# Attention and squared-ReLU MLP on one core: another order for the prologue, eight steps for the attention, loads issued before stores

## The chip, the cores and the metric

The kernel runs on one NeuronCore of one Trainium2 chip. The metric is device time in microseconds (us), lower is better; a run's time is a little longer than the span that its profile shows, since the span goes from the first to the last instruction.

## The reference

q, k and v are 8 x 8 x 576 x 64 (batch, heads, sequence, head size). Attention is local: the sequence is cut into chunks of 64, and a query sees the keys of its own chunk alone. The result, 4608 tokens of 512 channels, goes through an MLP with a squared ReLU:

```
scores = scale * q_c @ k_c^T          (per chunk of 64 and head)
attn   = exp(scores - max);  attn = attn / (sum + 1e-9)
x      = attn @ v_c                   -> (4608, 512)
h = x @ w_in (512 x 2048);  r = max(h, 0);  g = s * r*r + b
out = g @ w_out (2048 x 512)
```

All of it is in float32.

## The kernel before

The 4608 tokens are 36 token blocks (tb) of 128; four of them make a *block* of the outer loop, so there are nine blocks (L311). The hidden size 2048 is cut into 16 parts j. For each block and each j the kernel does an up-projection `up(j)` (L224: 12 matmuls 128 x 512 into one PSUM bank of the pool ps_h, which has two), on ScalarE and VectorE the square (L235) and the bias (L241), which leaves g as a high and a low part, and a down-projection `down(j)` (L248: 12 matmuls that accumulate in ps_o over all j). To keep float32 accuracy, x, the weights and g are each split into a high and a low part of type fp32r, and a product is three matmuls: high x high, low x high, high x low. `down` runs LAG = 2 steps behind `up`, so a block has 18 steps (L322), and `store` (L260) copies the four results out of PSUM on ScalarE and issues four stores on SP.

The weights arrive as 64-bit numbers, and the core converts them itself in block 0. The 32 weight tiles (up and down for each j) are put into 16 pairs (L61). A pair is loaded into one of three buffers of the pool raw; `scale` and `tail` (L87, L91) are on ScalarE, `bits` (L95) is two VectorE instructions (L98, L99) and one on GpSimd (L101), `hi` (L103) is on ScalarE and `lo` (L107, instruction L109) on VectorE. In block 0, step j does lo of pair j, tail and bits of pair j+2, hi of pair j+1, scale and load of pair j+3 (L330 to L343). The raw buffers are shared with the q and k of the attention, so a load waits until the buffer's earlier user has been read.

Attention is done two token blocks at a time, in a *group*: class Attention, L113. Its stages are load_qk, load_v, scores (64 matmuls of 64 x 64, L150), peak (L155), sub (L159), exp (L164), sum (L168), norm (reciprocal and product with it, L171 to L173, on VectorE), transposes (8 on TensorE, L180), copies (ScalarE, L185), values (64 matmuls, L191), x_hi (ScalarE, L201) and x_lo (VectorE, L205). A block needs two groups. While one block's MLP runs, the two groups of the next block are spread over its steps by a table, `plan` (L314 to L321): the key (j, 0) is ahead of up(j), (j, 1) behind up(j), and (j, 2) between the square and the bias of step j. The first group loads at (0, 0), has its scores at (1, 1), its product at (4, 2), transposes at (5, 1), values at (6, 1) and x_lo at (7, 2); the second group is seven steps later. One PSUM tile, ps_a, serves scores, transposes and values of a group in turn.

The first two groups (called one and two), and the first weight pairs, are done in a prologue (L272 to L308).

The order of the work is written out by hand: the pool manager runs with a manual schedule, each engine executes its instructions in the order of the program, and waits are put in where a tile's data or buffer needs them. All DMAs are issued on SP, in order; a DMA that has to wait holds every later one.

The lines that do this in the main loop:

```
for j in range(NJ + LAG):
    run(*plan.get((j, 0), ()))
    ...
layer.store()
```

Of the kernel before, what the change touches and what calls it, by code (L numbers as in the profile page):

```python
# [8 lines left out]
F32 = mybir.dt.float32  # L9
F32R = mybir.dt.float32r  # L10
U32 = mybir.dt.uint32
I32 = mybir.dt.int32
AF = mybir.ActivationFunctionType
ALU = mybir.AluOpType
# [4 lines left out]
def local_attention_then_squared_relu_mlp(ctx: ExitStack, tc, qkv, w, s, b, out):  # L19


    nc = tc.nc
    P = 128
    NTB, NJ = qkv.shape[0], w.shape[0]
# [18 lines left out]
    ps_h = ctx.enter_context(tc.tile_pool(name="ps_h", bufs=2, space=bass.MemoryType.PSUM))  # L43
# [8 lines left out]
    b_col = const.tile([P, 1], F32, name="b_col")  # L52
    ident = const.tile([P, P], F32, name="ident")
    make_identity(nc, ident)

# [6 lines left out]
    class Pair:  # L64
# [27 lines left out]
            _, low, _, _, _ = self.views(which)  # L92
            nc.scalar.activation(out=low.bitcast(I32), in_=low, func=AF.Copy, scale=2.0 ** -29)

        def bits(self, which=(0, 1)):  # L95
            f, low, high, _, _ = self.views(which)
            u, i = f.bitcast(U32), f.bitcast(I32)
            nc.vector.tensor_scalar(out=u, in0=u, scalar1=3, scalar2=None, op0=ALU.logical_shift_left)  # L98
            nc.vector.scalar_tensor_tensor(out=u, in0=high, scalar=0x80000000, in1=u,  # L99
                                           op0=ALU.bitwise_and, op1=ALU.bitwise_or)  # L100
            nc.gpsimd.tensor_tensor(out=i, in0=i, in1=low.bitcast(I32), op=ALU.add)  # L101

        def hi(self, which=(0, 1)):  # L103
            f, _, _, hi, _ = self.views(which)
# [102 lines left out]
    def block(tb0, bank):  # L207
        x = [xp.tile([P, NHP, 4 * P], F32R, name=n) for n in ("xh", "xl")]
        return x, [Attention(tb0 + i, x, i * P, bank) for i in range(0, 4, N)]
# [57 lines left out]
    def run(*steps):  # L267
        for f in steps:
            f()
# [3 lines left out]
    pair = [Pair(k) for k in range(NJ)]  # L273
# [7 lines left out]
    pair[2].load()  # L281
    nc.sync.dma_start(out=s_col, in_=s.unsqueeze(0).to_broadcast([P, 1]))
    nc.sync.dma_start(out=b_col, in_=b.unsqueeze(0).to_broadcast([P, 1]))
    run(one.scores, one.peak, one.sub, two.scores)
    pair[0].scale((0,))
    pair[0].tail((0,))
    one.exp()
    pair[0].bits((0,))
    run(one.sum, one.norm, one.transposes, two.peak, two.sub)
    pair[0].hi((0,))  # L290
    pair[0].scale((1,))
    pair[0].tail((1,))
    run(one.copies, one.values, two.exp)
    pair[0].lo((0,))
    pair[0].bits((1,))
    run(one.x_hi, two.sum, two.norm, two.transposes, one.x_lo)
    layer = Layer(0, x)
    first, second = slice(0, N * P), slice(N * P, 4 * P)
    layer.up(0, first)
    pair[0].hi((1,))  # L300
    run(two.copies, two.values)
    pair[0].lo((1,))
    pair[1].scale()
    pair[1].tail()
    pair[1].bits()
    layer.up(1, first)
    run(two.x_hi, two.x_lo)
    pair[2].scale()  # L308


    for tb0 in range(0, NTB, 4):  # L311


        plan = {}  # L314
        if tb0 + 4 < NTB:
            next_x, groups = block(tb0 + 4, steady_bank)
            for a, n in zip(groups, (1, 8)):
                for at, *fs in (((n - 1, 0), a.load_qk, a.load_v), ((n, 1), a.scores), ((n, 2), a.peak), ((n + 1, 2), a.sub),
                                ((n + 2, 0), a.exp), ((n + 2, 2), a.sum), ((n + 3, 2), a.norm), ((n + 4, 1), a.transposes),
                                ((n + 5, 0), a.copies), ((n + 5, 1), a.values), ((n + 6, 0), a.x_hi), ((n + 6, 2), a.x_lo)):  # L320
                    plan.setdefault(at, []).extend(fs)  # L321
        for j in range(NJ + LAG):  # L322
            run(*plan.get((j, 0), ()))
            if j < NJ:
                if tb0 or j > 1:
                    layer.up(j)
                else:
                    layer.up(j, second)
            run(*plan.get((j, 1), ()))
            if tb0 == 0:  # L330
                if j + 3 < NJ:
                    pair[j + 3].load()
                if 0 < j < NJ:
                    pair[j].lo()
                if j + 2 < NJ:
                    pair[j + 2].tail()
                    pair[j + 2].bits()
                if j + 1 < NJ:
                    pair[j + 1].hi()
            if j < NJ:  # L340
                layer.square(j)
            if tb0 == 0 and j + 3 < NJ:
                pair[j + 3].scale()  # L343
            run(*plan.get((j, 2), ()))
            if j < NJ:
                layer.bias(j)
            if j >= LAG:
                layer.down(j - LAG)
        layer.store()
        if tb0 + 4 < NTB:  # L350
            x = next_x
            layer = Layer(tb0 + 4, x)


# [29 lines left out]
```

## Time and profile before

| | |
|---|---|
| median of 3 runs | 897.93 us (896.51 to 898.06) |
| the profiled execution | 896.87 us, its span 895.1 us |
| mean granted TensorE clock | 0.996 |
| TensorE busy | 859.1 us (96% of the span) |
| VectorE / ScalarE / GpSimd busy | 375.9 / 308.7 / 39.8 us |
| DMA | 55.40 MB, 62 GB/s over the span |

In the rows, PE is TensorE, PEld its weight loads, DVE VectorE, ACT ScalarE, POOL GpSimd, and SPq the queue of SP, which issues the DMAs. A row of the timeline is: start (us), duration (us), engine, line of the kernel, operation, out<-in, shape, count, and in brackets the idle time of the engine just before it with what released it. Durations of a matmul hold its way through the array, so that matmuls overlap: twelve matmuls of 512 columns last 2.72 us from the first start to the next group's start.

### The profile page before, as it was taken

The numbers are of one execution on the slowest core, as the hardware profiler recorded it, in microseconds if no ns is written. First come the engines' busy times: TensorE is split into PE (matmuls) and PEld (weight loads), VectorE is DVE, ScalarE is ACT, GpSimd is POOL, SyncE is SP. The second block draws the span as 40 slices with busy tenths as digits, with TensorE's granted clock in tenths as the row PEclk, the third lists the DMA queues.
The fourth block names the chain that finished last, engine by engine and source line by source line (L and its number), as shares of the span: only waits on it lengthen the run. The fifth ranks groups of instructions, "written<-read, shape, count | busy, mean of one in ns | idle before, by whom it ended". The sixth has DMA issues, their size and how long they took to land.

```text
span 895.1 us, 13596 instructions
## 1 busy us (share of the span) xinstructions
PE 859.1 (96%) x5928; PEld 707.3 (79%) x5928; DVE 375.9 (42%) x483; ACT 308.7 (34%) x466; POOL 39.8 (4%) x23
## 2 busy tenths in 40 slices
PE   4789999999999999999999999999999999999997
PEld 3678787888788878888788878887888788888886
DVE  6698954342334334332534243433343343423221
ACT  4777743223332223232233233223322332322222
POOL 1333310000000000000000000000000000000000
PEclk9999999999999999999999999999999999999999
DMA  7556304000400040001200040004000400010001
GB/s 299 198 187 215 138 9 158 25 1 1 166 22 3 1 164 1 25 1 68 97 25 1 1 165 24 1 1 165 24 2 1 149 17 25 0 47 2 1 1 47
DMA packets 20507, 55.40 MB, mean 62 GB/s; under 512 B 2528, under 2 KB 2528, under 8 KB 20448
## 3 DMA queue, kind: packets, MB, share of 16 engines
q1 hardware_dynamic: 20448, 54.54, 16.8%
q8 instruction: 46, 0.75, 0.3%
q14 instruction: 13, 0.11, 0.0%
HBM read 45.09 MB, written 9.44 MB: 61 GB/s over the span
## 4 chain that ended last, share of the span: by engine, by line
PE 83%; DVE 7%; DMA 6%; ACT 2%; issue 1%; SPq 1%; POOL 0%; ACTq 0%; POOLq 0%
PE ps_o L257 42%; PE ps_h L231 36%; DMA raw<-in_qkv_dram 4%; PE ps_a L180 2%; PE ps_a L191 2%; PE ps_a L150 1%; DVE wp L109 1%; DMA raw<-in_w_dram 1%; DVE f L99 1%; ACT f L264 1%; DVE ps_h L239 1%; DVE f L98 1%; DVE g L245 1%; DVE p L173 1%; DVE z L171 1%
## 5 line engine op out<-in xcount | busy, mean ns | idle before, releaser
L257 PE MATMUL ps_o<-wp,g 128*128 128x512 f32 x1728 | 418.3, 393 | 0.0
L231 PE MATMUL ps_h<-xh,wp 128*128 128x512 f32 (+1 forms) x1168 | 380.9, 389 | 5.3 <-DVE g L245 5.0
L257 PEld LDWEIGHTS ps_o<-wp,g 128*128 128x128 f32 x1728 | 322.4, 188 | 67.1
L239 DVE SCALAR_TENSOR_TENSOR ps_h<-ps_h,s_col,r 128x512 f32<-128x512 f32 x144 | 109.1, 758 | 434.9 <-ACT r L238 434.9
L231 PEld LDWEIGHTS ps_h<-xh,wp 128*128 128x128 f32 x1168 | 219.6, 189 | 51.0 <-issue 4.8
L231 PE MATMUL ps_h<-xl,wp 128*128 128x512 f32 (+1 forms) x584 | 226.5, 388 | 0.8 <-DVE xl L205 0.8
L238 ACT ACTIVATE r<-ps_h 128x512 f32<-128x512 f32 x144 | 86.0, 597 | 387.8 <-PE ps_h L231 387.8
L244 ACT ACTIVATE g<-ps_h,b_col 128x512 fp32r<-128x512 f32 x144 | 99.2, 689 | 116.6 <-DVE ps_h L239 116.6
L245 DVE SCALAR_TENSOR_TENSOR g<-ps_h,b_col,g 128x512 fp32r<-128x512 f32 x144 | 107.4, 746 | 54.2 <-ACT g L244 54.2
L231 PEld LDWEIGHTS ps_h<-xl,wp 128*128 128x128 f32 x584 | 110.4, 189 | 23.0 <-DVE xl L205 1.0
L101 POOL TENSOR_TENSOR f<-f,raw 128x1024 int32<-128x1024 int32 (+1 forms) x17 | 39.1, 2300 | 78.1 <-DVE f L99 47.8
L264 ACT COPY f<-ps_o 128x512 f32<-128x512 f32 x36 | 19.4, 590 | 44.2 <-PE ps_o L257 44.2
L180 PE MATMUL ps_a<-ident,p 128*128 128x128 f32 x144 | 21.1, 295 | 10.6 <-DVE p L173 10.6
L180 PEld LDWEIGHTS ps_a<-ident,p 128*128 128x128 f32 x144 | 18.3, 153 | 13.5 <-issue 11.7
L150 PEld LDWEIGHTS ps_a<-raw 64*64 64x64 f32 x1024 | 17.2, 134 | 14.6 <-DMA raw<-in_qkv_dram 7.5
L150 PE MATMUL ps_a<-raw 64*64 64x64 f32 x1024 | 20.2, 222 | 8.0 <-DMA raw<-in_qkv_dram 7.6
L89 ACT ACTIVATE f<-raw 128x1024 f32<-128x1024 f32 (+1 forms) x17 | 18.6, 1094 | 15.6 <-DMA raw<-in_w_dram 11.9
L155 DVE TENSOR_REDUCE m<-ps_a 128x16 f32<-128x1024 f32 x16 | 19.5, 1219 | 7.8 <-PE ps_a L150 7.8
L109 DVE TENSOR_TENSOR wp<-f,wp 128x1024 fp32r<-128x1024 f32 (+1 forms) x17 | 22.3, 1313 | 0.0
L173 DVE TENSOR_TENSOR p<-p,z 128x1024 f32<-128x1024 f32 x18 | 22.0, 1224 | 0.6
L164 ACT ACTIVATE p<-p 128x1024 f32<-128x1024 f32 x18 | 19.1, 1061 | 8.3 <-DVE p L159 8.3
L168 DVE TENSOR_REDUCE z<-p 128x16 f32<-128x1024 f32 x18 | 21.8, 1209 | 0.1
(27 smaller groups left out, 216.3 us busy)
## 6 DMA issues: line engine op xcount, KB each, us to landing
raw<-in_w_dram SPq DMA_DIRECT2D x32, 512.0 KB, 4.4
raw<-in_qkv_dram SPq DMA_DIRECT2D x32, 512.0 KB, 5.5
out_dram<-f SPq DMA_DIRECT2D x36, 256.0 KB, 2.2
v<-in_qkv_dram SPq DMA_DIRECT2D x32, 256.0 KB, 4.3
wp<-in_qkv_dram SPq DMA_DIRECT2D x4, 512.0 KB, 5.2
wp<-in_qkv_dram SPq DMA_DIRECT2D x4, 256.0 KB, 8.2
s_col<-in_s_dram SPq DMA_DIRECT2D x1, 0.5 KB, 9.3
b_col<-in_b_dram SPq DMA_DIRECT2D x1, 0.5 KB, 8.2
```

The costliest lines, as they stand in the source:

```text
L101: nc.gpsimd.tensor_tensor(out=i, in0=i, in1=low.bitcast(I32), op=ALU.add)
L109: nc.vector.tensor_tensor(out=lo, in0=f, in1=hi.bitcast(F32), op=ALU.subtract)
L150: nc.tensor.matmul(out=self.ps[cols, c, i * NHP + hp, :], lhsT=qk[rows, 0, h, :], rhs=qk[rows, 1, h, :], start=True, stop=True)
L173: nc.vector.tensor_tensor(out=self.p3, in0=self.p3, in1=self.z.unsqueeze(2).to_broadcast([P, 2 * G, CH]), op=ALU.mult)
L180: nc.tensor.transpose(out=self.ps[:, i, hp * P:(hp + 1) * P], in_=p[:, g, :], identity=ident)
L231: nc.tensor.matmul(out=self.ps[j][:, cols], lhsT=w[:, c, :], rhs=x[:, c, :], start=(c == 0 and i == 0), stop=(c == NHP - 1 and i == 2))
L238: nc.scalar.activation(out=r, in_=ps, func=AF.Relu)
L239: nc.vector.scalar_tensor_tensor(out=ps, in0=ps, scalar=s_col, in1=r, op0=ALU.mult, op1=ALU.mult)
L244: nc.scalar.activation(out=gh, in_=ps, func=AF.Identity, bias=b_col)
L245: nc.vector.scalar_tensor_tensor(out=gl, in0=ps, scalar=b_col, in1=gh.bitcast(F32), op0=ALU.add, op1=ALU.subtract)
L257: nc.tensor.matmul(out=self.acc[t], lhsT=x[:, ts], rhs=w, start=(j == 0 and i == 0), stop=(j == NJ - 1 and i == 2))
L264: nc.scalar.copy(out=o[:, t % 2], in_=self.acc[t])
```

## The change

- A helper `keep_busy(n)` issues n identity products (128 x 128, identity times identity, float32) into a PSUM tile of the pool ps_h whose content nothing reads. The prologue has 39 of them in six places: 6 ahead of the first scores, 6 between the first and the second, 11 behind the second, 2 behind the first transposes, 12 behind the first values, 2 behind the second transposes.
- `bits` can be issued in two parts: L98 alone, or L99 with the GpSimd addition.
- The prologue has another order: pair 1's scale and tail come earlier; the second part of `bits` for the second half of pair 0 and its hi and lo come later; x_hi of group one comes before the sums of group two; copies, values and x_hi of group two come before up(0). The half of up(1) that the prologue did is gone, and up(1) is done whole in the loop.
- The plan of a group is eight steps long: norm moves from (n+3, 2) to (n+4, 0), the head of a step, and transposes, copies, values, x_hi and x_lo each come one step later. The second group starts at n = 9 in place of 8, so its x_lo is at (16, 2).
- The loads of a block's first group are taken out of step 0 and issued at the end of the block before (ahead of its stores), for the first of them at the end of the prologue.

```
+    busy = ps_h.tile([P, 4 * P], F32, name="ps_h")
+    def keep_busy(n):
+        for _ in range(n):
+            nc.tensor.matmul(out=busy[:, 0:P], lhsT=ident, rhs=ident, start=True, stop=True)
...
-        def bits(self, which=(0, 1)):
+        def bits(self, which=(0, 1), *half):
...
+            half = half or (0, 1)
+            if 0 in half:
+                nc.vector.tensor_scalar(out=u, in0=u, scalar1=3, ...)
+            if 1 in half:
+                nc.vector.scalar_tensor_tensor(out=u, in0=high, ...)
+                nc.gpsimd.tensor_tensor(out=i, in0=i, ...)
...
-    run(one.scores, one.peak, one.sub, two.scores)
+    keep_busy(6)
+    one.scores()
+    keep_busy(6)
+    two.scores()
+    keep_busy(11)
+    run(one.peak, one.sub)
     pair[0].scale((0,))
     pair[0].tail((0,))
     one.exp()
     pair[0].bits((0,))
     run(one.sum, one.norm, one.transposes, two.peak, two.sub)
+    keep_busy(2)
     pair[0].hi((0,))
     pair[0].scale((1,))
     pair[0].tail((1,))
-    run(one.copies, one.values, two.exp)
+    run(one.copies, one.values, two.exp, one.x_hi)
+    keep_busy(12)
     pair[0].lo((0,))
-    pair[0].bits((1,))
-    run(one.x_hi, two.sum, two.norm, two.transposes, one.x_lo)
+    pair[0].bits((1,), 0)
+    pair[1].scale()
+    pair[1].tail()
+    run(two.sum, two.norm, two.transposes, one.x_lo)
+    keep_busy(2)
+    pair[0].bits((1,), 1)
+    run(two.copies, two.values, two.x_hi)
+    pair[1].bits()
+    pair[0].hi((1,))
     layer = Layer(0, x)
     first, second = slice(0, N * P), slice(N * P, 4 * P)
     layer.up(0, first)
-    pair[0].hi((1,))
-    run(two.copies, two.values)
+    two.x_lo()
     pair[0].lo((1,))
-    pair[1].scale()
-    pair[1].tail()
-    pair[1].bits()
-    layer.up(1, first)
-    run(two.x_hi, two.x_lo)
     pair[2].scale()
...
+    def attention_plan(tb0):
+        x, groups = block(tb0, steady_bank)
+        plan = {}
+        for a, n in zip(groups, (1, 9)):
+            for at, *fs in (((n - 1, 0), a.load_qk, a.load_v), ((n, 1), a.scores), ((n, 2), a.peak), ((n + 1, 2), a.sub),
+                            ((n + 2, 0), a.exp), ((n + 2, 2), a.sum), ((n + 4, 0), a.norm), ((n + 5, 1), a.transposes),
+                            ((n + 6, 0), a.copies), ((n + 6, 1), a.values), ((n + 7, 0), a.x_hi), ((n + 7, 2), a.x_lo)):
+                plan.setdefault(at, []).extend(fs)
+        return x, plan, plan.pop((0, 0))
+    next_x, plan, loads = attention_plan(4)
+    run(*loads)
     for tb0 in range(0, NTB, 4):
...
-                if tb0 or j > 1:
+                if tb0 or j:
                     layer.up(j)
                 else:
                     layer.up(j, second)
...
-        layer.store()
+        previous, x, plan, loads = layer, next_x, {}, ()
         if tb0 + 4 < NTB:
-            x = next_x
             layer = Layer(tb0 + 4, x)
+        if tb0 + 8 < NTB:
+            next_x, plan, loads = attention_plan(tb0 + 8)
+        run(*loads)
+        previous.store()
```

More of the change, by code (lines that the diff above doesn't have):

```diff
@@ L93, in tail @@
             nc.scalar.activation(out=low.bitcast(I32), in_=low, func=AF.Copy, scale=2.0 ** -29)
-        def bits(self, which=(0, 1)):
+        def bits(self, which=(0, 1), *half):
             f, low, high, _, _ = self.views(which)
             u, i = f.bitcast(U32), f.bitcast(I32)
[L98 to L101, printed above, removed]
+            half = half or (0, 1)
+            if 0 in half:
+                nc.vector.tensor_scalar(out=u, in0=u, scalar1=3, scalar2=None, op0=ALU.logical_shift_left)
+            if 1 in half:
+                nc.vector.scalar_tensor_tensor(out=u, in0=high, scalar=0x80000000, in1=u,
+                                               op0=ALU.bitwise_and, op1=ALU.bitwise_or)
+                nc.gpsimd.tensor_tensor(out=i, in0=i, in1=low.bitcast(I32), op=ALU.add)
         def hi(self, which=(0, 1)):
@@ L299, in local_attention_then_squared_relu_mlp @@
     layer.up(0, first)
-    pair[0].hi((1,))
-    run(two.copies, two.values)
+    two.x_lo()
     pair[0].lo((1,))
-    pair[1].scale()
-    pair[1].tail()
-    pair[1].bits()
-    layer.up(1, first)
-    run(two.x_hi, two.x_lo)
-    pair[2].scale()
-    for tb0 in range(0, NTB, 4):
[L314 to L321, printed above, removed]
+    pair[2].scale()
+    def attention_plan(tb0):
[9 more added lines that the diff above has]
+    run(*loads)
+    for tb0 in range(0, NTB, 4):
         for j in range(NJ + LAG):
```

## The prediction

> **What bounds the kernel now.** I read the page first. TensorE is busy for 859.1 of 895.1 us, so about 36 us of idle time is all that a new order can win without removing work.
>
> ```profile
> span 895.1 us, 13596 instructions
> PE 859.1 (96%) x5928; PEld 707.3 (79%) x5928; DVE 375.9 (42%) x483; ACT 308.7 (34%) x466; POOL 39.8 (4%) x23
> ```
>
> Then TensorE's waits: who waited for whom, total us, times, longest.
>
> ```profile
> PE ps_a L180 <- DVE p L173: 10.6, 4, 3.4
> PE ps_a L150 <- DMA raw<-in_qkv_dram: 7.6, 11, 1.3
> PE ps_h L231 <- DVE g L245: 5.0, 2, 4.6
> ```
>
> The second row lies at the block boundaries, as the timeline at 706 us shows.
>
> ```profile
> 706.13 2.20 SPq L265 DMA_DIRECT2D out_dram<-f  x4
> 708.37 0.94 SPq L126 DMA_DIRECT2D raw<-in_qkv_dram  x2
> 714.40 0.69 PE L150 MATMUL ps_a<-raw 64*64 64x64 f32 x32 [1.21 <-DMA raw<-in_qkv_dram]
> ```
>
> SP issues the q and k loads only behind the four stores, which wait for the last copies of the block; the second half of the scores then waits for the landing. The chain of waits gives the block ends and the start of the third up-projection, up(2), at 715.09.
>
> ```profile
> 122.77 2.72 PE ps_h L231 x12
> 125.49 8.17 PE ps_o L257 x36
> 698.68 8.17 PE ps_o L257 x36
> 715.09 2.99 PE ps_h L231 x12
> 794.56 8.16 PE ps_o L257 x36
> ```
>
> Block ends are 133.66, 706.85 and 802.72, so seven blocks average 95.58 us. An undisturbed insertion of scores costs 1.18 us (from the end of the last up matmul, 752.55 + 0.23, to the next down):
>
> ```profile
> 752.55 0.39 PE L231 MATMUL ps_h<-xh,wp 128*128 128x512 f32 x1
> 753.96 3.02 PE L257 MATMUL ps_o<-wp,g 128*128 128x512 f32 x12
> ```
>
> The prologue, in order of time:
>
> ```profile
> 8.16 2.41 PE L150 MATMUL ps_o<-wp 64*64 64x64 f32 x64 [1.44 <-DMA wp<-in_qkv_dram]
> 13.51 1.94 PE L180 MATMUL ps_a<-ident,p 128*128 128x128 f32 x8 [2.95 <-DVE p L173]
> 15.49 1.22 DVE L159 TENSOR_TENSOR p<-ps_o,m 128x1024 f32<-128x1024 f32 x1 [0.99 <-PE ps_a L180]
> 18.18 1.07 ACT L201 CAST xh<-ps_o 128x512 fp32r<-128x512 f32 x2 [0.38 <-PE ps_o L191]
> 18.29 1.21 DVE L168 TENSOR_REDUCE z<-p 128x16 f32<-128x1024 f32 x1
> 18.51 1.27 POOL L101 TENSOR_TENSOR f<-f,raw 128x512 int32<-128x512 int32 x1 [6.76 <-DMA b_col<-in_b_dram]
> 21.28 1.28 DVE L205 TENSOR_TENSOR xl<-ps_o,xh 128x512 fp32r<-128x512 f32 x2
> 25.69 0.69 DVE L98 TENSOR_SCALAR f<-f 128x1024 uint32<-128x1024 uint32 x1 [2.54 <-ACT f L89]
> 27.78 2.45 POOL L101 TENSOR_TENSOR f<-f,raw 128x1024 int32<-128x1024 int32 x1 [8.00 <-ACT xh L201]
> 30.25 30.74 SPq L75 DMA_DIRECT2D raw<-in_w_dram  x14
> 35.22 1.12 ACT L89 ACTIVATE f<-raw 128x1024 f32<-128x1024 f32 x1 [3.41 <-DMA raw<-in_w_dram]
> 36.95 0.75 DVE L245 SCALAR_TENSOR_TENSOR g<-ps_h,b_col,g 128x512 fp32r<-128x512 f32 x1 [4.23 <-ACT g L244]
> 37.84 0.47 PE L231 MATMUL ps_h<-xh,wp 128*128 128x512 f32 x1 [4.65 <-DVE g L245]
> ```
>
> What ends last here is not TensorE. POOL's addition for weight pair 1 ends at 30.23 and frees a raw buffer; only then is pair 3 loaded; ACT holds pair 3's scaling in front of the bias of step 0, waits for the landing until 35.22, and the bias that frees PSUM for up(2) comes behind it. So up(2) starts 7.6 us after that addition ends, and matmuls made faster between 22 and 33 us would only lengthen the 4.65 us wait.
>
> In block 0 the first row of the waits has its other two places.
>
> ```profile
> 57.45 0.75 DVE L239 SCALAR_TENSOR_TENSOR ps_h<-ps_h,s_col,r 128x512 f32<-128x512 f32 x1
> 57.75 2.42 POOL L101 TENSOR_TENSOR f<-f,raw 128x1024 int32<-128x1024 int32 x1 [3.17 <-DVE f L99]
> 58.11 2.09 DVE L171 TENSOR_SCALAR z<-z 128x16 f32<-128x16 f32 x1
> 60.52 1.22 DVE L173 TENSOR_TENSOR p<-p,z 128x1024 f32<-128x1024 f32 x1
> 61.89 1.60 PE L180 MATMUL ps_a<-ident,p 128*128 128x128 f32 x8 [2.80 <-DVE p L173]
> 63.14 4.17 PE L257 MATMUL ps_o<-wp,g 128*128 128x512 f32 x12
> 106.72 1.06 PE L180 MATMUL ps_a<-ident,p 128*128 128x128 f32 x8 [1.42 <-DVE p L173]
> 107.16 1.21 DVE L109 TENSOR_TENSOR wp<-f,wp 128x1024 fp32r<-128x1024 f32 x1
> 112.33 1.66 DVE L109 TENSOR_TENSOR wp<-f,wp 128x1024 fp32r<-128x1024 f32 x1
> ```
>
> L171, 16 columns wide, takes 2.09 us because it ends with POOL's addition (57.75 + 2.42 = 60.17). The transposes wait 2.80 us, and behind that the clock is down: 4.17 us for 12 matmuls that otherwise take about 2.9, and 1.60 for 8 transposes that otherwise take 1.06. Busy time and granted clock (third number from the end) of one stretch behind the long wait of the prologue:
>
> ```profile
> 39.00:40.00 1.00, 1.00 (x3) 0.82 (x4) 0.96 (x2) 0.35 (x1) 0.00 (x0) 0.50 0.94 336
> ```
>
> After 4.65 us of idle the clock is 0.50; behind the wait of 1.42 the transposes take 1.06, so that one left it up.
>
> **Part 1, loads in front of stores.** Nothing is added; two q/k and two v loads move past four stores on SP. The q/k loads then wait only for a raw buffer whose readers ended steps before, so they are issued while the previous block runs. The v loads wait for that block's values at step 15, and behind them stand only the stores, whose copies come about 8 us later. The block that ends at 802.72 took 95.87 us, and from 706.85 to its up(2) at 715.09 went 8.24, where two ups and the scores need 2 x 2.72 + 1.18 = 6.62; without that 1.62 it is 94.25. Seven boundaries give 7 x (95.58 - 94.25) = 9.3 us. The waits row bounds it from below at 7.6; I take 9.3, since the block periods also hold what the gaps between modelled matmul ends lose. The next limit is PSUM for up(2), freed by the bias of step 0. The last block has no scores, and there up(2) waits for it 0.33 us:
>
> ```profile
> 808.49 0.50 PE L231 MATMUL ps_h<-xh,wp 128*128 128x512 f32 x1 [0.33 <-DVE g L245]
> ```
>
> Behind 1.18 us of scores it is 0.85 early.
>
> **Part 2, eight steps.** In steady blocks the product and the transposes had slack before, and no wait shows there: nothing won, nothing lost. The new last x products (group 2, step 16) lie under the last two downs, 5.4 us of TensorE; uncovered they would cost about 2.4 us (1.07 on ACT, 1.28 on DVE) per block end.
> In block 0 both waits go: 2.80 + 1.42, the slow down after the first (4.17 - 2.88 = 1.29) and its slow transposes (0.54), 6.1 us in all. What is late next is the lo of a weight pair (L109), since DVE now does the product ahead of it. On the old clock: square 57.45 to 58.2, the two bias steps (about 0.7 each) to 59.7, L171 held to 60.2, product to 61.74, lo to 62.9. The up that needs it would start at 61.8 and reach its third matmul at 62.2: about 0.8 us of wait. The next lo is held by POOL to about 67.3 and ends at 68.4 (in time); L98 and L99 (0.65, 1.23), square and bias follow to 71.75, then the first copy of the probabilities to 72.3, where up(7) ends at 71.6: the values wait 0.7. At the second product the lo by the same steps, 5.6 us each, ends near 111.5 and is wanted at 110.7: 0.8. So 2.3 us come back, and 3.8 remain. If lo had no effect it would be 6.1; if the waits merely moved (the 1.42 at both products and the 0.7), 2.6.
>
> **Part 3, the prologue.** Removed: the first half of up(1) as 12 matmuls of its own (up(1) is now 12 full ones). Moved: pair 0's second half behind x_lo of the first group, pair 1's scale and tail ahead of the second group's sums. Added: 39 identity products. The chain is DVE's, up to POOL's addition for pair 1:
> - transposes 13.51 to 14.55 if warm (1.06 as at 106.72, not 1.94): 0.9 earlier;
> - subtract, exponential, sum: from 14.6; the sum starts at 16.95 (before 18.29: L99 of pair 0 no longer precedes it and the exponential comes 0.9 earlier);
> - sum 1.21, normalisation 1.7, x_lo 1.28 to 21.1; L99 of half a pair (0.69) to 21.8;
> - L98 and L99 of pair 1 behind POOL's 1.27 for the half pair: both done at about 24.9 (before 27.65; scaling is no longer what they wait for, as it was at 25.69);
> - POOL 2.45 to 27.45, against 30.23.
>
> So up(2) comes 2.8 us earlier, at 35.0. With cold transposes it is 1.9. If L99 does not wait for POOL it is 4.0. TensorE still idles some 3.4 us ahead of up(2), and the low clock there stays, as does its cost.
>
> The price of an identity product is not in the trace. From below: a transpose of the same shape, about 0.13 warm and 0.24 cold (1.06 and 1.94 for 8). From above: a 128x512 matmul, 0.23 warm (2.72/12) and 0.43 at clock 0.50 (39 to 40 us). I take the transposes, the same shape and type: 39 x 0.13 to 0.24 = 5 to 9 us, all in stretches where TensorE idles. The eleven ahead of the first transposes matter: they start at 8.16 + 2.41 = 10.6 and end by 13.2 even cold, before 13.51. At the upper price the cover is gone (rival B).
> On warming: behind the wait of 2.80 the low clock cost 1.29 + 0.54 = 1.8 us, so at half speed it lasted some 3.7 us of work. The scores, six products and more scores keep TensorE at work from 4.3 to about 12, twice that, so I take the first transposes as warm. The Trainium skill (TensorE: Matmul & The Clock Gate, Part 1) puts the release at one busy window of about 3.4 us; by it they are warm too (2.8 us in this part, without it 1.9).
>
> **The sum.** 895.1 - 9.3 - 3.8 - 2.8 = 879.2 us span. The profiled run took 896.87, 1.8 more than its span: 881 us. That run lies 1.1 below the median of 897.93, inside the runs' 896.51 to 898.06.
>
> **The rivals.**
> A, as above: 881; chance 0.60.
> B, dear and cold identity products: six after the first scores (which end at 8.16 - 1.44 = 6.7) hold the second scores to 9.3, these take 2.4, eleven take 11 x 0.43 = 4.7 and end near 16.4, so the first transposes come 2.9 later instead of 0.9 shorter. For: the clock is slow at that time. Against: equal shapes in the transposes row. 881 + 0.9 + 2.9 = 885; 0.13. The Trainium skill (FP8 and Floating Point Precision, section TensorE Precision Notes) gives true FP32 four passes; that would make B's price the right one if the clock is still low; no run yet shows it.
> C, the loads come no earlier, because of a buffer still held: 881 + 9.3 = 890; 0.06. Against: the raw ring has three buffers and a group uses one.
> D, the other side: ACT takes the last x_hi behind the four store copies (the last two: 1.08 us from the block's end).
>
> ```profile
> 133.69 1.08 ACT L264 COPY f<-ps_o 128x512 f32<-128x512 f32 x2 [0.28 <-PE ps_o L257]
> ```
>
> Then x_hi and x_lo end about 1.1 + 1.07 + 1.28 = 3.5 us after the block's last down, and eight block starts lose 28 us: 881 + 28 = 909. It decides from 2 us per block (16/8). The written order puts x_hi two steps ahead of the copies, which speaks against; 0.04.
> E, POOL and DVE do not hold each other, and lo is never late: 881 - 1.2 - 2.3 = 877.5; 0.15. L171 (2.09) and L109 (1.66 against 1.21) speak against. The Trainium skill (SBUF — State Buffer, section Who interferes with whom) has the second of two such instructions blocked until the first ends, which these rows agree with.
> A remaining 0.02 is no change.
>
> Chances: faster by over 0.2% (about what can be told from no change here) A + B + C + E = 0.94; same 0.02; slower 0.04. The range 876 to 887 holds E, A and B, and leaves out C, D and no change.
>
> **What would show it.** Loads issued before the stores, no wait for in_qkv after the first block and a block period of about 94.3: part 1. No L173 wait in block 0, but waits for L109 near 60 us: part 2. First transposes near 1.1 us, POOL's pair 1 ending near 27.5, up(2) near 35: part 3. First transposes starting after 14 us would be B; a wait for xl at block starts, D.

## The result, and the profile after

The changed kernel takes 882.78 us (median of 4 runs, 880.81 to 883.22) against 897.97 for the kernel before (896.51 to 898.06, 4 runs): ratio 0.983, 95% interval 0.9812 to 0.9849, faster by 1.7%. Forecast were 881 us and a range of 876 to 887. The profiled execution has a span of 881.4 us, 13.7 less than before.

The page's first lines and TensorE's waits (who for whom, total us, times, longest) of the changed kernel:

```profile
span 881.4 us, 13719 instructions
PE 864.5 (98%) x5994; PEld 712.5 (81%) x5994; DVE 376.0 (43%) x483; ACT 308.2 (35%) x466; POOL 40.1 (5%) x23
```

```profile
PE ps_h L240 <- DVE g L254: 5.4, 2, 5.1
PE ps_h L240 <- DVE wp L118: 1.8, 2, 1.5
...
PE ps_a L200 <- ACT pT L194: 0.9, 1, 0.9
PE ps_a L189 <- DVE p L182: 0.8, 1, 0.8
```

The 7.6 us for q and k are gone, and of the 10.6 for the product 0.8 is left, in the prologue. The wait of up(2) for the bias (L254) did not shrink: its longest is 5.1, before 4.6. The waits for a weight pair's lo (L118) grew to 1.8, from 0.3 before, and the wait of the values in ps_a for the copies (L194) is new.

The chain of waits gives the block ends (start plus duration; first, second, eighth and last block):

```profile
121.51 8.39 PE ps_o L266 x36
...
215.63 8.39 PE ps_o L266 x36
...
780.35 8.39 PE ps_o L266 x36
...
868.24 8.17 PE ps_o L266 x36
```

Block 0 ends at 129.90 (before 133.66) and the eighth at 788.74 (802.72), so seven periods average 94.12 us (95.58). Of the 13.7 us, 7 x (95.58 - 94.12) = 10.2 come from the periods and 3.8 from the time up to the end of block 0; 0.3 is lost at the end of the kernel. At a boundary the timeline shows the loads far ahead of the stores, and scores that wait for nothing:

```profile
103.10 0.81 SPq L135 DMA_DIRECT2D raw<-in_qkv_dram  x2
...
129.19 2.19 SPq L274 DMA_DIRECT2D out_dram<-f  x4
...
135.26 1.16 PE L159 MATMUL ps_a<-raw 64*64 64x64 f32 x64
```

The prologue, in order of time:

```profile
1.36 2.93 PE L60 MATMUL ps_h<-ident 128*128 128x128 f32 x12 [1.36 <-POOL ident masks.py:199]
...
6.56 2.93 PE L60 MATMUL ps_h<-ident 128*128 128x128 f32 x12
...
9.41 1.61 PE L159 MATMUL ps_o<-wp 64*64 64x64 f32 x64
...
10.95 2.72 PE L60 MATMUL ps_h<-ident 128*128 128x128 f32 x22
...
13.51 1.04 PE L189 MATMUL ps_a<-ident,p 128*128 128x128 f32 x8
...
22.35 2.21 DVE L108 SCALAR_TENSOR_TENSOR f<-raw,f 128x1024 uint32<-128x1024 uint32 x1
...
23.50 1.45 SPq L135 DMA_DIRECT2D raw<-in_qkv_dram  x2
...
24.69 2.42 POOL L110 TENSOR_TENSOR f<-f,raw 128x1024 int32<-128x1024 int32 x1 [1.22 <-ACT wp L114]
...
33.79 1.12 ACT L95 ACTIVATE f<-raw 128x1024 f32<-128x1024 f32 x1 [5.11 <-DMA raw<-in_w_dram]
...
36.42 0.76 PE L240 MATMUL ps_h<-xh,wp 128*128 128x512 f32 x1 [5.07 <-DVE g L254]
```

Six identity products are 12 matmuls, eleven are 22: each product is two instructions. At the low clock the six take 2.93 us (0.49 each), at the full clock the eleven take 2.72 (0.25 each). Low and full are read here from the times of equal work. The clock column (third number from the end) does not show it: it is at 1.00 from the start, also inside the slow six:

```profile
8.00:9.00 1.00, 1.00 (x6) 1.00 (x6) 1.00 (x1) 0.00 (x0) 0.00 (x0) 1.00 1.00 404
```

The six hold the second scores, which began at 8.16 before, to 9.41; the clock rises while these run (1.61 us instead of 2.41), and the eleven end just where the transposes become ready. The transposes run in 1.04 us. POOL's addition for pair 1 ends at 27.11, before 30.23. But pair 3, loaded from then on, is scaled only at 33.79: 6.7 us after that addition, where it was 5.0. So up(2) starts at 36.42, 1.4 us earlier than before, not 2.8.

In block 0:

```profile
58.18 0.61 DVE L180 TENSOR_SCALAR z<-z 128x16 f32<-128x16 f32 x1
...
60.26 1.22 DVE L118 TENSOR_TENSOR wp<-f,wp 128x1024 fp32r<-128x1024 f32 x1
...
61.53 0.74 PE L240 MATMUL ps_h<-xh,wp 128*128 128x512 f32 x2 [0.30 <-DVE wp L118]
...
71.36 1.16 PE L200 MATMUL ps_a<-pT,v 64*64 64x64 f32 x64 [0.88 <-ACT pT L194]
...
89.31 1.13 ACT L95 ACTIVATE f<-raw 128x1024 f32<-128x1024 f32 x1 [3.04 <-DMA raw<-in_w_dram]
...
111.46 0.73 PE L240 MATMUL ps_h<-xh,wp 128*128 128x512 f32 x2 [1.51 <-DVE wp L118]
```

The small instruction at the head of the product takes 0.61 us instead of 2.09, and no transpose waits. In place of the old waits stand the three that had been forecast, of 0.30, 0.88 and 1.51 us. The last is the longest because ACT had to wait 3.04 us for weight pair 12 (89.31).

### The profile page after: what moved, and what is told of

Its sections match the earlier page's. It is cut to its first block, busy times and chain, and to the rows that moved or that the text cites. A ratio compares the mean times of both kernels' runs of the same rounds, so it can differ in the third digit from the quotient of the medians.

```text
span 881.4 us, 13719 instructions
## 1 busy us (share of the span) xinstructions
PE 864.5 (98%) x5994; PEld 712.5 (81%) x5994; DVE 376.0 (43%) x483; ACT 308.2 (35%) x466; POOL 40.1 (5%) x23
## 4 chain that ended last, share of the span: by engine, by line
PE 88%; DVE 6%; issue 2%; DMA 2%; ACT 1%; POOL 1%; SPq 0%; ACTq 0%; POOLq 0%
PE ps_o L266 41%; PE ps_h L240 40%; PE ps_a L200 2%; PE ps_a L159 2%; DVE wp L118 2%; PE ps_a L189 2%; DMA raw<-in_w_dram 1%; DVE ps_h L248 1%; DVE g L254 1%; DVE f L106 1%; PE ps_h L60 1%; ACT g L253 1%; DVE f L108 1%; POOL f L110 1%; DMA wp<-in_qkv_dram 0%
## 5 line engine op out<-in xcount | busy, mean ns | idle before, releaser
L254 DVE SCALAR_TENSOR_TENSOR g<-ps_h,b_col,g 128x512 fp32r<-128x512 f32 x144 | 107.6, 747 | 74.8 <-ACT g L253 74.8
L118 DVE TENSOR_TENSOR wp<-f,wp 128x1024 fp32r<-128x1024 f32 (+1 forms) x17 | 23.4, 1378 | 0.0
L200 PEld LDWEIGHTS ps_a<-pT,v 64*64 64x64 f32 x1024 | 16.4, 134 | 6.6 <-issue 4.9
L214 DVE TENSOR_TENSOR xl<-ps_a,xh 128x512 fp32r<-128x512 f32 x32 | 20.5, 683 | 1.7 <-ACT xh L210 1.7
L108 DVE SCALAR_TENSOR_TENSOR f<-raw,f 128x1024 uint32<-128x1024 uint32 (+1 forms) x17 | 20.7, 1220 | 0.5
L194 ACT COPY pT<-ps_a 128x512 f32<-128x512 f32 x36 | 19.2, 589 | 1.3 <-PE ps_a L189 1.3
```

What stands on the lines that cost most here:

```text
L118: nc.vector.tensor_tensor(out=lo, in0=f, in1=hi.bitcast(F32), op=ALU.subtract)
L200: nc.tensor.matmul(out=self.ps[cols, c, i * NHP + hp, :], lhsT=self.v[i][rows, h, :], rhs=self.pT[rows, i, hp, cols], start=True, stop=True)
L254: nc.vector.scalar_tensor_tensor(out=gl, in0=ps, scalar=b_col, in1=gh.bitcast(F32), op0=ALU.add, op1=ALU.subtract)
```

## The experiments

Each run's trace is read at the same marks: the start of up(2), the end of block 0, the mean of the seven following periods, the span.

| run | up(2) | block 0 ends | period | span | median |
|---|---|---|---|---|---|
| before | 37.84 | 133.66 | 95.58 | 895.1 | 897.97 |
| changed | 36.42 | 129.90 | 94.12 | 881.4 | 882.78 |
| loads only | 38.12 | 133.32 | 94.12 | 884.9 | 886.94 |
| eight steps only | 38.04 | 130.01 | 95.99 | 894.4 | 898.59 |
| old prologue | 37.96 | 130.09 | 94.12 | 881.6 | 883.38 |
| no products | 37.78 | 129.73 | 94.12 | 881.3 | 882.96 |
| 22 products | 37.99 | 131.11 | 94.12 | 882.7 | (884.47, one run) |
| product in its old place | 36.94 | 130.22 | 94.12 | 881.8 | (883.61, one run) |
| v behind pair 3 | 36.55 | 130.22 | 94.12 | 881.8 | 882.81 |
| v at step 2 | 36.66 | 128.97 | 94.12 | 880.7 | 882.61 |
| q, k, v behind pair 3 | 32.23 | 127.70 | 94.12 | 879.3 | 881.02 |
| changed, again | 36.52 | 128.65 | 94.12 | 880.3 | 882.07 |
| lo ahead of the product | 36.58 | 128.49 | 94.12 | 880.1 | 881.80 |
| pair 3 and lo first | 32.57 | 128.03 | 94.12 | 879.6 | 880.94 |

Medians of different rows come from up to four chips; on the chips of the experiments the kernel before took 902.03 us (loads only to no products), 899.98 (22 products, product in its old place, v behind pair 3, and q, k, v behind pair 3) and 901.52 (v at step 2 and the last three rows). The changed kernel's own two medians differ by 0.7 us, so a difference of that size between chips shows nothing.

**Each part alone.** First the loads, on the kernel before:

```
...
-        layer.store()
...
+        if tb0 + 8 < NTB:
+            next_x, plan, loads = attention_plan(tb0 + 8)   # the seven-step table
+        run(*loads)
+        previous.store()
...
```

> The kernel before with one part of the change: a group's first loads are issued at the end of the block before, ahead of the stores; prologue, seven-step attention and its tables stay. Theory: the shorter period of blocks 1 to 7 (95.58 to 94.12 us) comes from this part alone, so block 0 ends at 133.7 as before, the period is 94.1, and the span is 895.1 - 10.2 = 884.9 us. Rival: the eight steps bring a part of it, and the loads alone give the 7.6 us of the waits row: period 94.5, span 887.5.

The chain of waits of this run, first and eighth block:

```profile
125.16 8.16 PE ps_o L257 x36
...
784.00 8.16 PE ps_o L257 x36
```

From 133.32 to 792.16 are seven periods of 94.12 us, and the span is the 884.9 forecast. All of the shorter period comes from this part. Against the kernel before on the same chip the ratio is 0.9827 (0.98 to 0.9853): by the medians 15.1 us, since on that chip the kernel before was slower than in its profiled execution. So 10.2 us is what the part is worth against that execution, and against slower ones of the kernel before it is more.

Then the table alone: offsets (1, 9) and the new places of norm to x_lo in the kernel before.

> The kernel before with the eight-step table alone (product at a step's head, second group at step 9); loads behind the stores and prologue as before. Theory: only block 0 gains; up(2) stays at 37.8, block 0 ends 2.3 to 3.8 us earlier than 133.7 (2.3 in the whole change, 3.8 predicted), later blocks keep their 95.6, span 891.3 to 892.8. Rival: the waits only move from the transposes to the weight pairs' lo and to the values, less than 1 us is left, span 894 to 895.

```profile
121.61 8.40 PE ps_o L257 x36
...
793.57 8.39 PE ps_o L257 x36
```

Block 0 ends at 130.01, 3.65 us earlier: close to the 3.8 of the prediction, against the rival. The span fell by only 0.7, since this execution lost more at the boundaries (95.99 us per period, 95.58 before). The medians on one chip are 898.59 and 902.03, ratio 0.9954 (0.9927 to 0.9982).

Then both without the new prologue: the old lines from the first scores to pair 2's scale put back, `tb0 or j > 1` with them.

> The changed kernel with the prologue of before: no identity products, the old order, up(1) in two halves. Theory: the new prologue is worth the 1.4 us by which up(2) came earlier (37.84 to 36.42), so up(2) is back at 37.8 and the span is 881.4 + 1.4 = 882.8. Rival: block 0's later waits swallow it, since there the weight pairs and not TensorE set the end: span 881.4 to 881.8.

up(2) is back at 37.96, and yet block 0 ends at 130.09, 0.2 us behind the changed kernel: in these two executions the rival is right, the new prologue's 1.4 us are gone by the end of block 0. Up to the lo of weight pair 9 the changed kernel leads by 1.5 to 1.9 us. The lo of pair 10 stands behind the bias that ACT does after pair 12's scaling; that starts at 89.31 in the one and 89.30 in the other, and from there the two run 0.1 to 0.3 us apart. How much of that is chance is taken up under the landing of pair 12.

**The identity products.** Their loop body was taken out, and the PSUM tile that they wrote with it:

```
-    busy = ps_h.tile([P, 4 * P], F32, name="ps_h")
...
     def keep_busy(n):
-        for _ in range(n):
-            nc.tensor.matmul(out=busy[:, 0:P], lhsT=ident, rhs=ident, start=True, stop=True)
+        pass
```

> The changed kernel without the 39 identity products, everything else in place. Theory: the first transposes are slow (1.94 instead of 1.04 us) and stand on the chain, so POOL's addition for pair 1 ends 0.9 later (28.0 instead of 27.1) and up(2) starts near 37.3; span 882.3. Rival 1: the products are worth nothing, since the landing of pair 3 ends last for another reason: up(2) near 36.4, span 881.4. Rival 2: the products hold the second scores and more, and without them up(2) comes earlier than 36.4.

```profile
13.85 1.94 PE L187 MATMUL ps_a<-ident,p 128*128 128x128 f32 x8 [2.29 <-DVE p L180]
...
37.78 0.47 PE L238 MATMUL ps_h<-xh,wp 128*128 128x512 f32 x1 [3.57 <-DVE g L252]
```

The first transposes are slow again (1.94), and up(2) comes at 37.78: the products are worth 1.4 us there. At the end of block 0 (129.73) they are worth nothing against the changed kernel's first execution (129.90), but 1.1 us against its second (128.65, below), in which pair 12 landed after as short a time as here: 5.0 us from issue to scaling here (84.18 to 89.17), 5.2 there, 6.5 in the first. The median, 882.96, cannot be told from the changed kernel's 882.78; its second series, on yet another chip, has 882.07. Doubling the eleven:

```
-    keep_busy(11)
+    keep_busy(22)
```

> The changed kernel with 22 in place of 11 identity products ahead of the first transposes. A product is two matmul instructions of about 0.12 us each at the full clock, so 11 more take 2.7 us. Theory: the eleven end at 13.5, just where the transposes become ready, so the cover is used up and each further us is on the chain: transposes start near 16.2, POOL's addition for pair 1 ends near 29.8, up(2) near 39.1, span about 884. Rival: the wait ahead of up(2) covers it: up(2) 36.4, span 881.4.

```profile
6.78 1.60 PE L60 MATMUL ps_h<-ident 128*128 128x128 f32 x12
...
10.23 5.18 PE L60 MATMUL ps_h<-ident 128*128 128x128 f32 x44
...
15.24 1.04 PE L189 MATMUL ps_a<-ident,p 128*128 128x128 f32 x8
...
37.99 0.76 PE L240 MATMUL ps_h<-xh,wp 128*128 128x512 f32 x1 [4.87 <-DVE g L254]
```

The transposes start 1.7 us later and up(2) 1.6: the eleven had used the cover up, as the theory has it. In this execution the six products ahead of the second scores already ran fast (1.60 us in place of 2.93), so the 22 started at 10.23 and not 10.95: hence 1.7 and not 2.7.

**The place of the product.** Back to the slot between square and bias, with eight steps kept: `((n + 3, 2), a.norm)`.

> The changed kernel with the product of a group back between square and bias, a step's third slot, but still eight steps (transposes stay where the change has them). Theory: the place counts in block 0, where POOL adds at that time: L180 takes about 2 us instead of 0.6, the lo behind it ends about 0.7 later at both products, block 0 ends near 131.3 instead of 129.9; later blocks keep 94.1; span 882.8. Rival: only the added step counts: block 0 ends at 129.9, span 881.4.

```profile
57.21 2.12 DVE L180 TENSOR_SCALAR z<-z 128x16 f32<-128x16 f32 x1
```

The small instruction is held by POOL again: it ends at 59.33, where POOL's addition ends at 59.29 (56.85 + 2.44). From up(2) to the end of block 0 it takes 93.28 us, against 92.13 (128.65 - 36.52) in the execution of the changed kernel with an equally short landing of pair 12 (next but one paragraph): the place is worth about 1.1 us. That the added step is worth the rest is a subtraction, not a run.

**Why pair 3 lands late.** Three runs move the loads of block 1's first group. In the first, v is issued behind pair 3:

```
-    run(*loads)
+    run(loads[0])              # q and k alone
...
                     pair[j + 3].load()
+                    if j == 0:
+                        run(loads[1])
```

> The changed kernel with one pair of DMAs moved: the v loads (0.5 MB) of the first group of block 1 are issued behind pair 3's load instead of ahead of it. Theory: pair 3 lands 6.2 us after its issue, not 4.5, because the q, k and v loads issued at 23.5 to 25.9 still move then; without v, 0.5 MB at about 400 GB/s, it lands about 1.2 us earlier and up(2) starts near 35.2; span about 880.5. Rival: the landing is long for another reason (its own issue, the buffer): up(2) stays at 36.4, span 881.4.

up(2) is at 36.55: nothing, as the rival has it. In the second the condition is `j == 2`:

> The changed kernel with the v loads of block 1's first group issued at step 2 of block 0, after pair 3 has landed; they are not needed before step 7. With v behind pair 3 nothing was won, which fits two causes. Theory: what counts is the bytes under way between 24 and 33.7 us (q, k, v and pair 3, 2.6 MB), whatever their order of issue; with 0.5 MB fewer pair 3 lands 1.3 to 1.9 us earlier and up(2) starts near 34.8. Rival: q and k alone, or the time at which they are issued, make the landing long: up(2) stays near 36.4.

```profile
26.83 6.74 SPq L81 DMA_DIRECT2D raw<-in_w_dram  x6
...
33.61 1.42 SPq L145 DMA_DIRECT2D v<-in_qkv_dram  x2
34.03 1.12 ACT L95 ACTIVATE f<-raw 128x1024 f32<-128x1024 f32 x1 [5.66 <-DMA raw<-in_w_dram]
```

Pair 3, issued at 26.83, is scaled at 34.03, 7.2 us later, with v issued only at 33.61. So the bytes of v are not the cause, and my theory falls; up(2), at 36.66, is where the rival has it, which puts it on q and k or on the time of issue. In the third, q, k and v stand behind pair 3, which then takes the buffer that is free first; the scores of that group go one step later:

```
+            d = int(tb0 == 4 and n == 1)
-            ((n, 1), a.scores), ((n, 2), a.peak), ((n + 1, 2), a.sub), ...
+            ((n + d, 1), a.scores), ((n + d, 2), a.peak), ((n + 1 + d, 2), a.sub), ...
...
-    run(*loads)
...
                     pair[j + 3].load()
+                    if j == 0:
+                        run(*loads)
```

> The changed kernel with q, k and v of the first group of block 1 loaded behind pair 3, which so takes the raw buffer that is free first (23.5 instead of 27.1); that group's scores, peak, subtraction, exponential and sum come one step later. Theory: the wait for pair 3 ends the prologue's chain, so pair 3 lands near 28.5, the bias of step 0 no longer waits for it, and up(2) starts near 31.5; the next limit is pair 4, whose buffer comes free near 32 and which lands near 36.6, so of the 5 us about 1.5 to 2 stay: span about 879.5. Rival: the raw ring gives the whole back: span 881.4; or the late scores cost more than it brings.

```profile
23.77 1.79 SPq L81 DMA_DIRECT2D raw<-in_w_dram  x2
...
29.59 1.14 ACT L95 ACTIVATE f<-raw 128x1024 f32<-128x1024 f32 x1 [0.62 <-DMA raw<-in_w_dram]
...
32.23 0.47 PE L240 MATMUL ps_h<-xh,wp 128*128 128x512 f32 x1 [1.64 <-DVE g L254]
...
37.99 1.14 ACT L95 ACTIVATE f<-raw 128x1024 f32<-128x1024 f32 x1 [4.07 <-DMA raw<-in_w_dram]
```

up(2) starts 4.2 us earlier, at 32.23, and the next limit is pair 4, as forecast: ACT waits 4.07 us for it. Of the 4.2 us 1.0 to 2.2 are left at the end of block 0 (127.70 against 128.65 and 129.90), span 879.3. Pair 3 still takes 5.8 us from issue to scaling, with no earlier load under way. In the last run below, where it stands at the same place, it takes 6.6:

```profile
23.36 0.80 SPq L81 DMA_DIRECT2D raw<-in_w_dram  x2
...
29.93 1.14 ACT L95 ACTIVATE f<-raw 128x1024 f32<-128x1024 f32 x1 [1.38 <-DMA raw<-in_w_dram]
```

So loads ahead of it, v or q and k, are not needed to make it late. The time of its issue alone does not do it either: it takes 6.8 and 6.5 us where it is issued at 28.35 (no products) and 28.87 (22 products). What no run separates is this: in all ten runs with the new prologue the first q and k load is issued 3.6 us before or behind pair 3, which takes 5.8 to 7.2 us, and in the four with the old prologue 10.4 us before it, and it takes 5.0 to 5.1. Whether loads that share the time are the cause, or something else in the new prologue, stays open.

**The landing of pair 12.** The changed kernel unaltered:

> The changed kernel once more. In the traces so far pair 12 of block 0 lands either about 5.0 us after its load is issued (without the identity products, with the old prologue, with the old place of the product) or about 6.5 us (the changed kernel, v behind pair 3, 22 products), and block 0 ends about 1.4 us later with the long landing. Theory: which of the two it is is chance, so one more execution may show 5.0 and a block end near 128.5 (span 880.0), or 6.5 and 129.9 again. Rival: it belongs to the changed kernel's own timing: 6.5 and 129.9.

```profile
88.05 1.15 ACT L95 ACTIVATE f<-raw 128x1024 f32<-128x1024 f32 x1 [1.59 <-DMA raw<-in_w_dram]
```

Here pair 12 is scaled at 88.05, not 89.31, and block 0 ends at 128.65, not 129.90, with up(2) at the same place (36.52 and 36.42). So the landing differs between two executions of one kernel (on two chips), and that is worth 1.25 us. The run with the old prologue had the short landing too (84.40 to 89.30, 4.9 us); against it, the new prologue does leave a gain: 130.09 - 128.65 = 1.4 us. On this chip the changed kernel takes 0.9793 (0.9756 to 0.983) of the time of the kernel before.

**The lo ahead of the product.** In the same step norm goes behind the weight pair's lo:

```
-                            ((n + 2, 0), a.exp), ((n + 2, 2), a.sum), ((n + 4, 0), a.norm), ...
+                            ((n + 2, 0), a.exp), ((n + 2, 2), a.sum), ((n + 4, 3), a.norm), ...
...
                     pair[j].lo()
+            run(*plan.get((j, 3), ()))
+            if tb0 == 0:
```

> The changed kernel with the product of a group behind the lo of the weight pair instead of ahead of it, in the same step. Theory: what the two up-projections wait for in block 0 (0.30 and 1.51 us by the waits) is that lo, held by the product; with lo ahead both waits go. The first is given back at the values, which wait for copies; of the second about 0.9 us stays: block 0 ends near 129.0 with the long landing of pair 12 (127.6 with the short one), span 880.5 (879.1). Rival: bits and lo come so close that the wait moves on whole: 129.9.

```profile
PE ps_a L200 <- ACT pT L194: 1.9, 2, 1.7
...
PE ps_h L240 <- DVE wp L118: 0.4, 1, 0.4
```

Pair 12 landed short here too (scaled at 88.24), so the changed kernel's second execution is the one to compare with. There the waits for lo were 0.5 in all and the one for the copies 0.9; here they are 0.4 and 1.9. Block 0 ends at 128.49, 0.16 earlier: the first wait moves on to the copies, as the rival has it, and the second was hardly there to be won. My 0.9 us were wrong. The two edits together:

> The two edits that won or should win, together: pair 3 loaded ahead of q, k and v, and the lo ahead of the product. Theory: they act at different places (up(2) at 32.2 instead of 36.4, and the waits at the two products), so block 0 ends 0.9 us earlier than 127.7: 126.8, span 878.4. Rival: weight pair 12 or another load then ends last, and the block end stays at 127.7, span 879.3.

128.03 and 880.94 us: no more than pair 3 first alone (127.70; 881.02 on another chip). On the same chip the changed kernel took 882.07 (881.72 to 882.51) and this one 880.94 (880.01 to 881.39), 1.1 us less. That is the lowest median, a gain of 0.13%; it cannot be told from that of pair 3 first alone.

## Why the prediction was right, and where not

**Loads in front of stores** (9.3 forecast, 10.2 measured): right, and shown alone. The bias path is free early enough, and no buffer holds the loads (rival C). The unit was 0.13 us too long per period: I worked out 94.25 from one boundary, and 94.12 is measured.

**Eight steps** (3.8 forecast): 3.65 with the table alone, and 133.32 - 130.09 = 3.2 us between the runs with and without it where the loads are already in front. The forecast waits came where they were put: lo at the first product (0.30 against 0.8), the copies two steps later (0.88 against 0.7), lo at the second product (1.51 against 0.8). The second is long only where pair 12 lands late; in the second execution both waits for lo together are 0.5.

**The prologue** (2.8 forecast): 1.4 at up(2), and 0.2 to 1.4 at the end of block 0. The step that failed is "So up(2) comes 2.8 us earlier, at 35.0". The part up to POOL's addition was right (27.11 against 27.45, the transposes warm at 1.04). The 7.6 us from there to up(2) were taken over as a constant, and they were 9.3: the load in between took 1.7 longer. I had counted what each moved step does on the engines, and had put at nothing that the load might take longer in its new place. Why it does is open.

**The price of an identity product** was wrong on both sides: 0.49 us at the low clock and 0.25 at the full, above my upper ends of 0.43 and 0.23, because a product is two instructions, where a transpose of the same shape and type is one (8 for 8 in the row of 13.51). So B's price was right and its clock was not: the clock rose at about 10 us (an estimate, from scores that take 1.61 us between 2.41 slow and 1.16 fast), in time for the eleven. "End by 13.2 even cold" did not hold: they ended at about 13.5, and warm. That they were in time was luck, since at 0.49 us each eleven would take 5.4 us (an estimate). That rival deserved more than 0.13.

On the warming, the first transposes are warm (1.04 us), as I drew from the Trainium skill (TensorE: Matmul & The Clock Gate, Part 1). The trace does not agree with its busy window of about 3.4 us: matmuls follow each other almost without a gap from 1.36 us on, and the slow rate lasts to about 10 us, so nearly 9 us. It is not the same in every execution: of the nine with the products, the second six ran slow in four (2.93 us) and fast in five (1.60), and those behind the second scores fast in all. What the warming is worth here is 1.4 us at up(2), measured by taking the products out.

**The low clock at up(2)** stayed, as forecast, and came sooner: the granted clock is 0.50 from 36 us on, where before it was 0.68 between 38 and 39 and 0.50 only from 39. From up(2) to the first down it takes 5.15 us (36.42 to 41.57), before 4.77 (37.84 to 42.61).

**Rivals D and E** did not occur. No wait for x stands at a block's start. E needed that L108 and L118 are not held by POOL; in the changed prologue L108 of pair 1 takes 2.21 us, next to POOL's addition, where it took 1.23 before.

The sum: 9.3 + 3.8 + 2.8 = 15.9 forecast, 13.7 measured in the profiled execution. The loads gave 0.9 more; up to the end of block 0 it was 3.8 instead of 6.6; and 0.3 went at the end of the kernel. That the forecast came so near is in part luck, since the first two errors have opposite signs.

## What to carry to other kernels

Read from the timeline which queue entry stands in front of the load that a stage waits for; moving the load ahead of a store that waits for the last result was worth 10.2 of 13.7 us here, and no run shows a cost. Where a chain goes through a DMA, its landing is not a constant: moving the steps ahead of it also moves the time of issue and what shares the time with it, and here the same load took 5.0 us with one order and 5.8 to 7.2 with the other. A gain at one mark must be followed to the next place where something else ends last: 4.2 us won at up(2) were 1 to 2 us at the end of block 0, since the next weight pair was then the late one.

## What the runs showed that I had not expected

An identity product of 128 x 128 in float32 is two matmul instructions (78 more for 39 products, 12 fewer for up(1): 5928 to 5994), where 64 x 64 scores are one each. The same products and scores ran slow to about 10 us in four executions, and in five others they were fast at 6.8 us or before. The load of pair 3 took 5.0 to 5.1 us until its data were used with the old prologue and 5.8 to 7.2 with the new. And the loads behind the stores made the kernel before uneven: on one chip its 11 runs went from 899.69 to 906.36 us, and the 4 of the kernel with the loads moved, and nothing else, from 886.65 to 887.17.
